# Late-query attention first in alternating pairs, and six blocks of layer one moved behind the attention at 512 tokens beside layer two's weight conversion

## The chip, the core and the metric

The kernel runs on one core of one Trainium2 chip. Its engines are TensorE (PE: matmuls, and the weight loads PEld that overlap them), VectorE (DVE), ScalarE (ACT), GpSimd (POOL) and SyncE (SP), which issues DMAs. Each runs its own queue of instructions in order; they meet through semaphores. The metric is the device time of the whole program in microseconds (us), the median of several executions. "L883" is line 883 of the kernel's file.

## What is computed

Attention with a memory term, causal, on four batches and eight heads, then two feed-forward layers on the 2304 tokens that come out. All data are float32, the weights of the two layers arrive as float64.

```python
# q, k, v: (4, 8, 576, 64)
scores = where(causal, -1e9, q @ k.T / 8);  a = softmax(scores)
local = a @ v
q_p = elu(q) + 1
mem_out = (q_p @ M_prev) / (q_p @ z_prev + 1e-6)
attn = g * mem_out + (1 - g) * local            # g = sigmoid(beta), by head
x = attn as (2304, 512)
h = x @ moe_w_in;   x = maximum(0.01 * h, h) @ moe_w_out       # layer one, 512 -> 2048 -> 512
h = x @ moe2_w_in;  out = (h - tanh(h)) @ moe2_w_out           # layer two, the same sizes
```

## The kernel before

**Attention** is cut into 32 units (class Unit, L453): two heads of one batch, with the first 256 queries (kind A, "early", 256 keys) or the last 320 (kind B, "late", all 576 keys). A unit's steps are: load of qk and v; the memory term (L546, finished by L565 and added by TensorE at L706); scores on TensorE (L608, and L613 for the last 64 queries) into PSUM tiles "s"; maxima with the mask on VectorE (L634), which also writes the scores to tiles "e"; exponentials on ScalarE (L654); scaling by the row sums (L688 to L692); transposes on TensorE (L740, L728) and copies to "pt"; the values on TensorE (L762) into PSUM "o". Four units of one kind and batch fill a block "x" of 256 tokens; the 64 queries left over of each batch make a ninth block, "R". Each "e" tile has one buffer, so a unit's scores find a place when the unit before has been transposed.

**A layer** multiplies a block by w_in (up), applies the activation and multiplies by w_out (down). Each float32 operand is held as two fp32r parts, high and low, and a product is three matmuls (high x high, high x low, low x high). The float64 weights come as pairs of 32-bit words; `convert` (L795) makes float32 of them with one magnitude on ScalarE (L820) and four VectorE instructions (L823, L826, L831, L836), then for layer one a high copy (L435, L437) and a low part (L448). Layer one's weights are 32 tiles of 512 KB. Layer two's are converted in 64 chunks of 256 columns into a DRAM scratch (vscr), and later reloaded and split.

**Layer one** is narrow: 256 tokens a time, a "pair" of two weight tiles being 24 up (L883) and 24 down matmuls (L985) with the leak (L962) between, eight pairs per block. The first four blocks go in two sweeps (SWEEPS; 2 pairs, then 6), with partial sums in DRAM, since their weights are not all there yet. Layer one's matmuls fill TensorE between the units' steps.

**What sets the order.** Nothing is ordered by the hardware but by the program's text, and that text comes from a planner (class Schedule): each step is an operation with its possible engines, its cost and its priority, and the planner plays the engines forward on these costs and emits what is ready. Units have the priority of their number; the weights' conversions are set between units by W1_FROM and W2_FROM; layer one takes what is left. RINGS gives the number of buffers.

**Layer two** is wide: a loop written by hand, 512 tokens a round (four rounds and one half round for R), one item per weight tile: 12 up matmuls of 512 columns (L1180), the activation on ScalarE and VectorE (L1148 to L1160), a high copy (L1167) and a low part on GpSimd (L448), and, three items later, 12 down matmuls (L1206). It begins when all of layer one is done.

Of the kernel before, what the change touches and what calls it, by code (L numbers as in the profile page):

```python
# [40 lines left out]
STEP = 8  # L41

FINE = (0, 0, 0, 0, 16, 48, 24, 40, 8, 32, 20, 28, 36)

APART = (160, 192, 160, 192, 192)
# [3 lines left out]
CALM = 6000.0  # L49

# [47 lines left out]
class Schedule:  # L98


    def __init__(self, rings):
        self.rings = {k: [None] * n for k, n in rings.items()}
        self.count = {k: 0 for k in rings}
        self.made = {k: 0 for k in rings}
        self.ops = []
        self.lanes, self.sent, self.landed = [0.0] * LANES, 0, 0.0

# [50 lines left out]

    def send(self, t, sizes):

        for size in sizes:
            k = self.sent % LANES
            t = max(t, self.lanes[k])
            took = size / 375.0
            self.landed = self.lanes[k] = max(self.landed + max(180.0, took), t + 2000.0 + took)
# [4 lines left out]
    def run(self):  # L170
# [13 lines left out]
        cold, mode = 0.0, 0  # L184
# [3 lines left out]
        while todo:  # L188
# [6 lines left out]
            while again:  # L195
                again = False
                for e in engines:
                    if free[e] > t:
                        continue
                    for i, (_, _, at, o) in enumerate(ready[e]):  # L200
# [12 lines left out]
                        if e == "pe":  # L213
# [3 lines left out]
                            if t > free[e] + 700.0:  # L217
                                cold = t
                            if t < cold + 3600.0:
                                mine += o.alts[e] + 90.0  # L220
# [40 lines left out]
CW = 256  # L261
# [9 lines left out]
W1_FROM, W1_STEP = (3.7, 15.7), 0.002  # L271

SPLIT = 4

CUT = 2
W2_FROM, W2_STEP = 14, 0.25
# [3 lines left out]
def kernel(  # L280
# [80 lines left out]

    chunks = [(m, f, c) for p in range(NP) for m in range(2) for f in (2 * p, 2 * p + 1) for c in range(512 // CW)]

# [15 lines left out]
    groups = [(k, b) for k in "AB" for b in range(B)]  # L379
# [13 lines left out]
    xsv = [dram.tile([128, KT, 256], F32, name=f"xsv{n}") for n in range(SPLIT)]  # L393
    xps = [dram.tile([128, KT, 256], F32, name=f"xps{n}") for n in range(SPLIT)]
    x8s = dram.tile([128, KT, 256], F32, name="x8s")

# [24 lines left out]
    x_h, mz_h = {}, {}  # L421
    w_h = [[sc.new(None) for f in range(NF)] for m in range(2)]
# [3 lines left out]
    xv_h = [sc.new(None) for n in range(NBLK)]  # L426
    xp_h = [[sc.new(None) for i in range(2)] for n in range(NBLK)]

    SWEEPS = [(n, 0, CUT) for n in range(SPLIT)] + [(n, CUT, NP) for n in range(SPLIT)]
    SWEEPS += [(n, 0, NP) for n in range(SPLIT, NBLK)]  # L430
# [22 lines left out]
    class Unit:  # L453
# [14 lines left out]
        def declare(self, pr, prev):  # L468
# [25 lines left out]
            fresh_mz = (kind, b) not in mz_h  # L494
            if fresh_mz:
                mz_h[kind, b] = new("mz")
            mz = mz_h[kind, b]
# [790 lines left out]
```

## Time and profile before

| | us |
|---|---|
| median of 3 runs | 1050.04 |
| lowest and highest | 1049.82, 1052.98 |
| the profiled execution | 1052.7 |
| its span, first to last instruction | 1051.0 |
| PE busy in the span | 1017.6 |
| DVE, ACT, POOL busy | 733.1, 615.4, 104.8 |
| first wide matmul of layer two | at 654.05 |

Busy times are sums over the span; a stretch with its own limit is read from the view by stretches. The durations of neighbouring instructions on an engine can overlap, so their starts tell what one costs. A view's "releaser" is what ended an engine's idle time.

### The profile page before, as it was taken

The numbers are of one execution on the slowest core, as the hardware profiler recorded it, in microseconds if no ns is written. First come the engines' busy times: TensorE is split into PE (matmuls) and PEld (weight loads), VectorE is DVE, ScalarE is ACT, GpSimd is POOL, SyncE is SP. The second block draws the span as 40 slices with busy tenths as digits, with TensorE's granted clock in tenths as the row PEclk, the third lists the DMA queues.
The fourth block names the chain that finished last, engine by engine and source line by source line (L and its number), as shares of the span: only waits on it lengthen the run. The fifth ranks groups of instructions, "written<-read, shape, count | busy, mean of one in ns | idle before, by whom it ended". The sixth has DMA issues, their size and how long they took to land.

```text
span 1051.0 us, 18406 instructions
## 1 busy us (share of the span) xinstructions
PE 1017.6 (97%) x6816; PEld 881.0 (84%) x6816; DVE 733.1 (70%) x1718; ACT 615.4 (59%) x1298; POOL 104.8 (10%) x111
## 2 busy tenths in 40 slices
PE   5789998999999999999999999999999999999998
PEld 3678897877779977989999999888888888888897
DVE  7999997786776667763212257788687687777765
ACT  6888875667562256553101123776676676676664
POOL 1000100000000000000000000222222222222221
PEclk9899999999999999999999999999999999999999
DMA  9765625544644354332100046000100010010010
GB/s 256 233 191 164 219 100 156 167 124 129 187 120 153 110 149 131 114 89 67 41 1 21 1 161 198 23 21 1 61 21 1 36 46 1 0 61 1 1 41 20
DMA packets 93866, 95.06 MB, mean 90 GB/s; under 512 B 45392, under 2 KB 69968, under 8 KB 93776
## 3 DMA queue, kind: packets, MB, share of 16 engines
q1 hardware_dynamic: 92560, 92.58, 28.9%
q10 hardware_dynamic: 1216, 1.31, 0.4%
q8 instruction: 53, 0.87, 0.3%
q14 instruction: 37, 0.30, 0.1%
HBM read 71.32 MB, written 22.54 MB: 89 GB/s over the span
## 4 chain that ended last, share of the span: by engine, by line
PE 76%; DMA 5%; ACT 2%; DVE 1%; issue 0%; SPq 0%; ACTq 0%
PE up L1180 19%; PE dn L1206 19%; PE dn L985 14%; PE up L883 14%; PE s L740 3%; PE o L762 3%; PE s L608 2%; DMA cv<-in_moe_w_in_dram 2%; PE s L613 1%; DMA qk<-in_qkt_dram 1%; PE s L546 1%; DMA vs<-cv 1%; PE o L706 1%; DMA cv<-in_moe_w_out_dram 1%; ACT cv L820 0%; PE s L728 0%
## 5 line engine op out<-in xcount | busy, mean ns | idle before, releaser
L883 PE MATMUL up<-xs,w 128*128 128x256 f32 x1728 | 233.4, 286 | 1.2 <-ACT g L962 1.2
L883 PEld LDWEIGHTS up<-xs,w 128*128 128x128 f32 x1728 | 216.2, 191 | 6.4 <-issue 5.0
L1180 PE MATMUL up<-xs,w 128*128 128x512 f32 (+1 forms) x960 | 207.7, 367 | 0.0
L1180 PEld LDWEIGHTS up<-xs,w 128*128 128x128 f32 x960 | 167.7, 188 | 30.4
L1206 PE MATMUL dn<-w,gh 128*128 128x512 f32 x576 | 174.9, 389 | 0.0
L985 PE MATMUL dn<-gh,w 128*128 128x256 f32 x1152 | 159.5, 284 | 0.3 <-DVE gh L437 0.3
L985 PEld LDWEIGHTS dn<-gh,w 128*128 128x128 f32 x1152 | 144.3, 189 | 4.8 <-issue 4.8
L448 POOL TENSOR_TENSOR gl<-gf,gh 128x512 fp32r<-128x512 f32 x71 | 92.0, 1296 | 485.9 <-ACT gh L1167 485.9
L1157 DVE SCALAR_TENSOR_TENSOR gf<-u,w 128x512 f32<-128x512 f32 x72 | 83.7, 1163 | 68.1 <-ACT w L1154 68.0
L962 ACT ACTIVATE g<-up 128x512 f32<-128x512 f32 x72 | 42.6, 594 | 144.6 <-PE up L883 138.6
L1206 PEld LDWEIGHTS dn<-w,gh 128*128 128x128 f32 x576 | 107.6, 188 | 21.8
L1206 PE MATMUL dn<-w,gl 128*128 128x512 f32 x288 | 109.5, 389 | 0.0
L654 ACT ACTIVATE e<-e,mx 128x128 f32<-128x128 f32 (+4 forms) x144 | 82.9, 578 | 18.7 <-DVE mx L634 10.7
L1148 ACT ACTIVATE u<-up 128x512 f32<-128x512 f32 x72 | 42.9, 596 | 79.5 <-PE up L1180 79.5
L985 PE MATMUL dn<-gl,w 128*128 128x256 f32 x576 | 82.7, 282 | 0.0
L437 DVE CAST gh<-g 128x512 fp32r<-128x512 f32 x32 | 13.7, 427 | 90.7 <-ACT g L962 90.7
L985 PEld LDWEIGHTS dn<-gl,w 128*128 128x128 f32 x576 | 73.4, 188 | 2.8 <-issue 2.8
L634 DVE CUSTOM_DVE_ANT_0 e<-s,mask 128x128 f32<-128x128 f32 (+4 forms) x144 | 64.0, 483 | 16.5 <-PE s L608 12.7
L740 PE MATMUL s<-identr,e 128*128 128x128 f32 x448 | 65.4, 284 | 7.8 <-DVE e L690 3.3
L435 ACT ACTIVATE pt<-s 128x320 f32<-128x320 f32 (+4 forms) x147 | 57.2, 435 | 18.7 <-PE s L740 10.2
L1206 PEld LDWEIGHTS dn<-w,gl 128*128 128x128 f32 x288 | 54.1, 188 | 11.4
L740 PEld LDWEIGHTS s<-identr,e 128*128 128x128 f32 x448 | 52.5, 145 | 12.3 <-ACT pt L435 4.4
(98 smaller groups left out, 1382.0 us busy)
## 6 DMA issues: line engine op xcount, KB each, us to landing
w<-in_moe_w_out_dram SPq DMA_DIRECT2D x16, 512.0 KB, 5.0
cv<-in_moe_w_in_dram SPq DMA_DIRECT2D x32, 256.0 KB, 2.8
vs<-cv SPq DMA_DIRECT2D x64, 128.0 KB, 1.8
cv<-in_moe_w_out_dram SPq DMA_DIRECT2D x32, 256.0 KB, 3.0
w<-vs SPq DMA_DIRECT2D x32, 256.0 KB, 2.8
w<-in_moe_w_in_dram SPq DMA_DIRECT2D x14, 512.0 KB, 5.1
qk<-in_qkt_dram SPq DMA_DIRECT2D x16, 448.0 KB, 3.8
v<-in_v_dram SPq DMA_DIRECT2D x16, 320.0 KB, 3.5
```

Source lines behind the costliest of these rows:

```text
L435: nc.scalar.activation(out=out, in_=in_, func=AF.Copy)
L448: (nc.vector if e == "dve" else nc.gpsimd).tensor_tensor(out=out, in0=in_, in1=high, op=ALU.subtract)
L634: nc.vector.tensor_tensor_reduce(out=out, in0=in0, in1=in1, scale=-scale, scalar=mx.tile[:, 0:1] if t == 4 and j else BIG, op0=ALU.add, op ...
L654: nc.scalar.activation(out=x, in_=x, func=AF.Exp, scale=-1.0, bias=mx.tile[:, k:k + 1], accum_out=sm.tile[:, 2 * i + j:2 * i + j + 1])
L740: nc.tensor.transpose(ss[j].tile[:, a:a + 128], x, ident)
L883: nc.tensor.matmul(ps()[:, s, :], lhsT=w[:, wh * 512 + kt * 128:wh * 512 + (kt + 1) * 128], rhs=xs()[:, xh, kt, :], start=(kt == 0 and j = ...
L962: nc.scalar.activation(out=g.tile, in_=ps.tile.rearrange("p a b -> p (a b)"), func=AF.Prelu, alpha=0.01)
L985: nc.tensor.matmul(dn[m // 2].tile[:, m % 2, :], lhsT=w[:, wh * 512 + m * 128:wh * 512 + (m + 1) * 128], rhs=gg.tile[:, s * 256:(s + 1) * ...
L1148: nc.scalar.activation(out=u, in_=h, func=AF.Square)
L1157: nc.vector.scalar_tensor_tensor(out=g, in0=u, scalar=lin, in1=w, op0=ALU.mult, op1=ALU.add)
L1180: nc.tensor.matmul(ps[:, s * n:(s + 1) * n], lhsT=w[:, wh * 512 + kt * 128:wh * 512 + (kt + 1) * 128], rhs=xs[:, xh, kt, 0:n], start=(kt = ...
L1206: nc.tensor.matmul(dn, lhsT=g[:, c0:c0 + 128], rhs=wt[1][f][:, wh * 512:(wh + 1) * 512], start=(fs[0] == 0 and s == 0 and j == 0), stop=(f ...
```

## The change

The units' list (UNITS) has the late kind first, then the early one, and the blocks are numbered in that order: B0 to B3, A0 to A3, R. The late units of batch 0 and all early units alternate between two sets of "e" tiles; the late ones' second set lies in three weight tiles (LENT) that are loaded later. The first six units (LEND) put their scores into layer one's PSUM tiles "up" and "dn" instead of "s".

Only three blocks (NARROW: B0, B1, B2) go through layer one narrow, in one sweep each. The other six are stored (x1s), and the hand-written loop gets three wide rounds of layer one before layer two's five. In the first 32 of their 48 items, two chunks of layer two's weights per item are loaded (`fetch`) and converted (`refine`) into the scratch; in the last 16 each weight tile is reloaded and split (`reload`) as soon as its last use is past. The planner's own clock model and DMA costs are changed too (pace, send), with W1_FROM, which sets the conversions of weight tiles 1 to 8 against the units.

```diff
-W1_FROM, W1_STEP = (3.7, 15.7), 0.002
-SPLIT = 4
+W1_FROM, W1_STEP = (7.7, 15.7), 0.002
+NARROW = 3
+LEND = 6
+LENT = ((0, 15), (1, 15), (1, 14))
+UNITS = [(k, b, hp, hp % 2 if k == "A" or b < 1 else 0) for k in "BA" for b in range(4) for hp in range(4)]
...
             for tiles in ([[0, 1]] if kind == "A" else [[2], [3], [4]]):
-                ss = [new("s"), new("s")]
+                if not self.lend:
+                    ss = [new("s"), new("s")]
+                elif tiles == [3]:
+                    ss = [new("dn0"), new("dn1")]
+                else:
+                    ss = [new("up"), new("up")]
...
-                    et[t - q0] = new(f"e{t if t > 1 or self.hp % 2 else t + 2}")
+                    if kind == "A":
+                        et[t - q0] = new(f"e{t if self.alt else t + 2}")
+                    else:
+                        et[t - q0] = new(f"{'h' if self.alt else 'e'}{t}")
...
+        if n >= NARROW:
+
+            def save_x(e):
+                nc.sync.dma_start(out=x1s[n], in_=x.tile)
+
+            sop([("sp", 600)], save_x, reads=[x], writes=[x1_h[n]], dma=[-524288])
+            return
...
-    for i, (m, f, c) in enumerate(chunks):
-        convert(m, f, c, 1, (0, 100 + i), [ends[min(int(W2_FROM + i * W2_STEP), len(ends) - 1)]])
-    for i, sweep in enumerate(SWEEPS):
-        layer1(i, *sweep)
+    for n in range(NBLK - 1):
+        layer1(n)
...
-    WIDE = SPLIT
-    rounds = [(2 * r, 2 * r + 1) for r in range(WIDE)] + [(NBLK - 1,)]
+    rounds = [(1, (NARROW + 2 * r, NARROW + 2 * r + 1)) for r in range((NBLK - NARROW) // 2)]
+    FIRST2 = len(rounds)
+    rounds += [(2, (2 * r, 2 * r + 1)) for r in range(NBLK // 2)] + [(2, (NBLK - 1,))]
...
+    def act1(i):
+        h = state.pop((2, i, "up"))
+        g = t_p.tile([128, 512], F32, name="gf")
+        nc.scalar.activation(out=g, in_=h, func=AF.Prelu, alpha=0.01)
+        if "late" in state:
+            act2_end(*state.pop("late"))
+        yield
+        state["late"] = (i, g)
...
+                    if layer == 1:
+                        lhs, rhs = w[:, wh * 512 + k * 128:wh * 512 + (k + 1) * 128], g
+                    else:
+                        lhs, rhs = g[:, c0:c0 + 128], w[:, wh * 512:(wh + 1) * 512]
...
+    def reload(m, f, step):
+
+        w = wt[m][f]
+        if step == 0:
+            nc.sync.dma_start(out=w.bitcast(F32)[:, 512:1024], in_=vscr[m][f])
+        else:
+            copy("act", w[:, 0:512], w.bitcast(F32)[:, 512:1024])
+            low("dve" if m else "pool", w[:, 512:1024], w.bitcast(F32)[:, 512:1024], w.bitcast(F32)[:, 0:512])
+
+    def fetch(j):
+        m, f, c = chunks[j]
+        raw = t_p.tile([128, 512], I32, name=("u", "hu")[j % 2])
+        w_load(raw, (w2_in, w2_out)[m], m, f, c, 256, nc.sync)
+        state["raw", j] = raw
+
+    def refine(j):
+        m, f, c = chunks[j]
+        raw = state.pop(("raw", j))
+        g = t_p.tile([128, 512], F32, name=("w", "mk")[j % 2])
+        for step in (c_abs, c_max, c_shift, c_high, c_low):
+            step(raw[:, :], g[:, 0:256])
+        nc.sync.dma_start(out=vscr[m][f][:, c * 256:(c + 1) * 256], in_=g[:, 0:256])
...
     for i in range(len(items) + LAG2):
...
+        for j in range((i + 1) * EACH, min((i + 2) * EACH, len(chunks))):
+            fetch(j)
+        for j in range(i * EACH, min((i + 1) * EACH, len(chunks))):
+            refine(j)
+        for turn in turns.get(i, ()):
+            reload(*turn)
```

How the instructions stand after the change, at three places. In a row, "x9" counts neighbours of the same form, the names are the output's and the inputs' tiles with a number of their making, and "128x256" is partitions by elements. In the kernel after, L910 and L988 are the narrow up and down (L883, L985 before), L647 and L652 the scores, L567 the memory term, L745 its addition, L779 and L767 the transposes, L801 the values, L1163 and L1200 the wide up and down.

TensorE around its first matmul of layer one, before (the values and transposes of early units, then the first up matmuls of weight tile 0):

```order
L762 MATMUL o<-pt,va 64x256 x2
L762 MATMUL o<-pt,va 64x128 x2
L740 MATMUL s<-identr,e_497 128x128
L740 MATMUL s<-identr,e_501 128x128 x2
L740 MATMUL s<-identr,e_497 128x128
L740 MATMUL s<-identr,e_501 128x128 x2
L883 MATMUL up<-xs,w_0_258 128x256 x9
L546 MATMUL s<-mz_168,ph 128x130 x2
L883 MATMUL up<-xs,w_0_258 128x256 x3
L883 MATMUL up<-xs,w_1_311 128x256 x12
```

Ahead of this piece stand only the first early units. TensorE at the same point after the change:

```order
L647 MATMUL up<-qk 128x384 x2
L647 MATMUL dn_928<-qk 128x512
L647 MATMUL dn_929<-qk 128x512
L767 MATMUL s<-identr,e_715 128x128
L567 MATMUL s<-mz_165,ph 128x130 x3
L652 MATMUL up<-qk 64x288 x4
L801 MATMUL o<-pt,v 64x320 x6
L801 MATMUL o<-pt,v 64x192 x2
L801 MATMUL o<-pt,v 64x64 x2
L910 MATMUL up<-xs,w_0_273 128x256 x9
L745 MATMUL o<-identr,mo 128x128 x3
L910 MATMUL up<-xs,w_0_273 128x256 x3
```

Before, 48 rows of attention stand ahead of the first up row, all of early units; now 138 rows do, those of five late units up to their values and the scores of the sixth, which go into "up" and "dn".

VectorE beside a late unit's maxima (L634 before, L673 after; "ISA e,mx" is a maximum), before, in the late half of the attention:

```order
L690 TENSOR_SCALAR e_3357<-e_3357,sm 128x576
L538 SCALAR_TENSOR_TENSOR ph<-qk,ph 128x320
L823 TENSOR_SCALAR cv<-cv 128x256
L826 TENSOR_SCALAR cv<-cv 128x256
L831 SCALAR_TENSOR_TENSOR cv<-cv 128x256
L634 ISA e_3490,mx<-s,mask 128x384
L634 ISA mx 128x1
L634 ISA e_3490,mx<-s,mask 128x384
L634 ISA mx 128x1
L836 SCALAR_TENSOR_TENSOR cv<-cv 128x256
```

The conversions between are chunks of layer two (256 columns). VectorE at a late unit's maxima after the change, in the first half of the attention (L841, L844, L849 and L854 are the conversion's four instructions, L468 the low part):

```order
L673 ISA e_1366,mx<-s,mask 128x384
L673 ISA mx 128x1
L673 ISA e_1366,mx<-s,mask 128x384
L673 ISA mx 128x1
L468 TENSOR_TENSOR w_6_1377<-cv,w_6_1377 128x512
L844 TENSOR_SCALAR cv<-cv 128x512
L841 TENSOR_SCALAR cv<-cv 128x512
L849 SCALAR_TENSOR_TENSOR cv<-w_7_878,cv 128x512
L709 SCALAR_TENSOR_TENSOR sm<-sm,omg_72 128x2
L844 TENSOR_SCALAR cv<-cv 128x512
L714 RECIPROCAL sm<-sm 128x2
L854 SCALAR_TENSOR_TENSOR cv<-w_7_878,cv 128x512
```

A late unit's own instructions are the same ones; beside them stand layer one's weight tiles (512 columns), all 32 by the twelfth unit's maxima, and no chunk of layer two anywhere in the attention.

TensorE at the end of the narrow layer one, after:

```order
L988 MATMUL dn_3965<-gl,w_15_2332 128x256 x2
L988 MATMUL dn_3978<-gl,w_15_2332 128x256 x2
L1163 MATMUL up<-xs,w_0_273 128x512 x12
L1163 MATMUL up<-xs,w_1_401 128x512 x12
L1163 MATMUL up<-xs,w_2_581 128x512 x12
L1163 MATMUL up<-xs,w_3_614 128x512 x12
L1200 MATMUL dn_5020<-gh,w_0_404 128x512 x2
L1200 MATMUL dn_5020<-gl,w_0_404 128x512
L1200 MATMUL dn_5021<-gh,w_0_404 128x512 x2
L1200 MATMUL dn_5021<-gl,w_0_404 128x512
L1200 MATMUL dn_5022<-gh,w_0_404 128x512 x2
L1200 MATMUL dn_5022<-gl,w_0_404 128x512
```

The last narrow down rows are followed by four groups of 12 wide up matmuls, and then by the wide down matmuls, in which a piece of the weight is the stationary operand; before, at this place, layer two's wide rounds began.

## Rows read from the trace of the kernel before

**Rows 1.** The page: busy time of two engines; granted clock in 40 slices, in tenths.
```profile
PE 1017.6 (97%) x6816; PEld 881.0 (84%) x6816; DVE 733.1 (70%) x1718; ACT 615.4 (59%) x1298; POOL 104.8 (10%) x111
...
PEclk9899999999999999999999999999999999999999
```

**Rows 2.** Stretches: length, busy PE, PEld, DVE, ACT, POOL (instructions), granted clock, DMA share, GB/s.
```profile
0.00:654.05 654.05, 625.04 (x4993) 552.56 (x4994) 440.52 (x1338) 343.57 (x846) 12.75 (x40) 0.99 0.43 130
0.00:78.00 78.00, 57.57 (x397) 45.76 (x397) 71.36 (x270) 62.08 (x183) 5.93 (x17) 0.93 0.79 229
26.00:52.00 26.00, 19.99 (x144) 16.09 (x141) 25.92 (x97) 21.84 (x65) 1.24 (x2) 0.87 0.79 234
...
78.14:109.86 31.72, 31.72 (x277) 27.76 (x276) 30.69 (x119) 26.80 (x83) 2.44 (x5) 1.00 0.51 148
195.51:260.00 64.49, 63.77 (x495) 50.14 (x494) 46.91 (x163) 45.43 (x114) 0.46 (x3) 1.00 0.49 141
654.05:1051.00 396.95, 392.56 (x1824) 328.48 (x1823) 292.58 (x380) 271.78 (x453) 92.03 (x71) 1.00 0.07 24
```

**Rows 3.** The same for narrow up matmuls alone (L883): PE, PEld, clock, DMA.
```profile
78.14:109.86 31.72, 11.17 (x75) 9.46 (x75) 1.00 0.51 148
195.51:260.00 64.49, 19.43 (x120) 15.84 (x120) 1.00 0.49 141
```

**Rows 4.** The same for narrow down matmuls alone (L985).
```profile
78.14:109.86 31.72, 8.29 (x60) 7.46 (x60) 1.00 0.51 148
195.51:260.00 64.49, 13.97 (x103) 12.65 (x102) 1.00 0.49 141
```

**Rows 5.** The chain that ended last: start, us, what; narrow, then wide.
```profile
483.92 2.80 PE dn L985 x24
486.72 2.80 PE up L883 x24
...
645.48 2.91 PE up L883 x24
...
664.96 2.72 PE dn L1206 x12
667.68 2.72 PE up L1180 x12
```

**Rows 6.** Timeline of VectorE: start, us, instruction.
```profile
139.51 0.69 DVE L836 SCALAR_TENSOR_TENSOR cv<-w,cv 128x512 int32<-128x512 int32 x1
140.11 0.69 DVE L448 TENSOR_TENSOR gl<-g,gh 128x512 fp32r<-128x512 f32 x1
140.72 0.42 DVE L826 TENSOR_SCALAR cv<-cv 128x512 int32<-128x512 int32 x1
141.05 0.69 DVE L448 TENSOR_TENSOR w<-cv,w 128x512 fp32r<-128x512 f32 x1
```

**Rows 7.** Groups of VectorE by form: count, busy us, mean ns, idle before.
```profile
L634 DVE CUSTOM_DVE_ANT_0 e<-s,mask 128x512 f32<-128x512 f32 x32 | 20.9, 686 | 1.7 <-PE s L608 1.5
...
L675 DVE RECIPROCAL sm<-sm 128x1 f32<-128x1 f32 x16 | 2.5, 159 | 0.2
```

**Rows 8.** Groups by form: leak, magnitude, one conversion, low part on GpSimd.
```profile
L962 ACT ACTIVATE g<-up 128x512 f32<-128x512 f32 x72 | 42.6, 594 | 144.6 <-PE up L883 138.6 <-DMA x2s<-g 5.5 <-DVE pt L437 0.2
...
L820 ACT ACTIVATE cv<-cv 128x256 f32<-128x256 f32 x64 | 27.7, 433 | 56.4 <-DMA cv<-in_moe_w_in_dram 25.8 <-DMA cv<-in_moe_w_out_dram 21.3 <-DVE gl L448 2.3
...
L831 DVE SCALAR_TENSOR_TENSOR cv<-cv 128x256 int32<-128x256 int32 x64 | 27.2, 424 | 1.5
...
L448 POOL TENSOR_TENSOR gl<-gf,gh 128x512 fp32r<-128x512 f32 x71 | 92.0, 1296 | 485.9 <-ACT gh L1167 485.9
```

**Rows 9.** Timeline of TensorE: a late unit's transposes that waited.
```profile
288.68 0.98 PE L740 MATMUL s<-identr,e 128*128 128x128 f32 x7 [1.77 <-ACT e L688]
```

**Rows 10.** Timeline of TensorE: six transposes at two times near the start.
```profile
39.48 1.75 PE L740 MATMUL s<-identr,e 128*128 128x128 f32 x6 [3.09 <-DVE e L690]
...
50.19 0.82 PE L740 MATMUL s<-identr,e 128*128 128x128 f32 x6
```

More of the change, by code (lines that the diff above doesn't have):

```diff
@@ L106, in __init__ @@
         self.lanes, self.sent, self.landed = [0.0] * LANES, 0, 0.0
+        self.speed, self.until, self.work = 0.5, 700.0 + WINDOW, []
     def new(self, tag):
@@ L157, in room, with pace @@
         return True
+    def pace(self, t):
+        while self.until <= t:
+            lo = self.until - WINDOW
+            busy = sum(min(b, self.until) - max(a, lo) for a, b in self.work if b > lo and a < self.until)
+            self.work = [x for x in self.work if x[1] > self.until]
+            if busy > 0.9 * WINDOW:
+                self.speed = 1.0
+            elif busy < 0.5 * WINDOW:
+                self.speed = 0.5
+            self.until += WINDOW
+        return self.speed
     def send(self, t, sizes):
@@ L376, in pool_copy @@
         nc.gpsimd.tensor_scalar(out=out, in0=in_, scalar1=1.0, scalar2=0.0, op0=ALU.mult, op1=ALU.add)
-    groups = [(k, b) for k in "AB" for b in range(B)]
+    groups = []
+    for u in UNITS:
+        if u[:2] not in groups:
+            groups.append(u[:2])
+    groups.sort(key=lambda g: max(i for i, u in enumerate(UNITS) if u[:2] == g))
     blocks = groups + [("R", 0)]
@@ L425 @@
     x2_h = [sc.new(None) for n in range(NBLK)]
[L426 to L430, printed above, removed]
+    x1_h = {n: sc.new(None) for n in range(NARROW, NBLK - 1)}
+    x1_h[NBLK - 1] = x8_h
     seqs = [0]
@@ L869, in convert, with w_lo @@
+        def w_lo(e):
+            w = wt[m][f]
+            low(e, w[:, 512:1024], g.tile, w.bitcast(F32)[:, 0:512])
+        op(copies(512), w_hi, reads=[g], writes=[wh])
+        op(lows(512), w_lo, reads=[g, wh], writes=[wh])
         return first
@@ L1049 @@
     ends = []
-    for kind, b in groups:
-        for hp in range(H // 2):
-            u = Unit(kind, b, hp)
-            u.declare((0, u_at), prev)
-            prev = u
-            u_at += 1
-            ends.append(sc.ops[-1])
+    for kind, b, hp, alt in UNITS:
+        u = Unit(kind, b, hp)
+        u.alt, u.lend = alt, u_at < LEND
+        u.declare((0, u_at), prev)
+        prev = u
+        u_at += 1
+        ends.append(sc.ops[-1])
     att_ops = list(sc.ops)
@@ L1087, in load2 @@
         x = late["x2"].tile([128, KT, 256], F32, name="x2i")
[L1088 removed]
+        layer, parts = rounds[r]
+        nc.sync.dma_start(out=x, in_=(x1s if layer == 1 else x2s)[parts[i]])
         state[2, r, i, "x"] = x
@@ L1184, in token_tiles @@
     def token_tiles(r):
-        return [(n, t) for n in rounds[r] for t in range(2)]
+        return [(n, t) for n in rounds[r][1] for t in range(2)]
     def out_copy(r, k):
-        n, t = token_tiles(r)[k]
+        layer, parts = rounds[r]
         last = r == len(rounds) - 1
@@ L1196, in down2 @@
         r, fs = items[i]
+        layer = rounds[r][0]
         if fs[0] == 0:
@@ L1213, in down2 @@
                 out_copy(r, k)
-    items = [(r, (f,)) for r in range(WIDE) for f in range(NF)]
-    items += [(WIDE, (2 * p, 2 * p + 1)) for p in range(NP)]
+    items = [(r, (f,)) for r in range(len(rounds) - 1) for f in range(NF)]
+    items += [(len(rounds) - 1, (2 * p, 2 * p + 1)) for p in range(NP)]
     def prep2(r, step):
-        if r + 1 < len(rounds) and step // 2 < len(rounds[r + 1]):
+        if r + 1 < len(rounds) and step // 2 < len(rounds[r + 1][1]):
             i = step // 2
@@ L1231 @@
             up2(i)
-            steps = act2(i)
+            r, fs = items[i]
+            steps = act1(i) if rounds[r][0] == 1 else act2(i)
             next(steps)
```

259 lines of the change are left out of this document (112 added, 147 removed), and 2 rows, old and new, of the table RINGS.

## The prediction

> **What bounds the kernel now.** I read the page's busy times first, then the view by stretches, then single rows. The page [rows 1] has TensorE at 97% of the span, with no other engine over 70%, and its line of granted clock is at full speed but for one or two slices at the start. The stretches [rows 2] say where the other 3% lie. Up to 654.05 us (attention and layer one) TensorE is busy 625.04, so 29.0 us are idle; 20.4 of these lie in the first 78 us, where VectorE is busy 71.4 of 78.0. From 654 on (layer two, 512 tokens wide) 392.6 of 397.0 are busy. So a gain must come from fewer TensorE microseconds, or from the start.
>
> What the units cost TensorE follows from one stretch of each kind, cut at the start of a unit's values. From 195.51 to 260.00 there are four late units, and in the same stretch 120 narrow up and 103 narrow down matmuls [rows 2 to 4]. A narrow matmul goes by at 2.80/24 = 0.1167 us [rows 5] (the printed duration is longer, since they overlap), so (64.5 - 0.7 idle - 223 x 0.1167)/4 = 9.4 us for a late unit. From 78.14 to 109.86 there are five early units and 135 narrow matmuls: (31.7 - 15.8)/5 = 3.2. The attention is then 16 x 9.4 + 16 x 3.2 = 202 us; a block's layer one is 8 x 48 x 0.1167 = 44.8, nine are 403. Together 605: of the 654 us 49 are lost, 29 to idling and some 20 to a low clock, to broken rows of matmuls and to my rounding.
>
> VectorE needs the same care. Its printed durations overlap: 139.51, 140.11, 140.72 and 141.05 are successive starts, so a row of 0.69 costs 0.60 and one of 0.42 costs 0.335 [rows 6], 0.085 less than printed. A weight tile of layer one is 2 x 0.335 + 3 x 0.60 = 2.47. A late unit has 15 groups of instructions of its own, 114.5 us in 310 over 16 units, of which the first and the last stand in [rows 7]: (114.5 - 310 x 0.085)/16 = 5.5, with a copy now and then 5.6.
>
> **The change part by part.**
> (1) Six blocks pass layer one wide. A wide group of 12 takes 2.72, so 0.2267 a matmul [rows 5]. One 512-token round is 16 x 5.44 = 87.0, three are **261.1**; narrow, the same six blocks are 6 x 44.8 = 268.8. The gain is 7.7, up to 3.5 more where groups take 2.91 instead of 2.80, as the row at 645.48.
> The Trainium skill's "TensorE: Matmul & The Clock Gate", section "Wait — 56ns, not 53.3ns?", gives N/2.4 GHz plus about 2.5 ns from start to start. By it a pair of 256 columns costs 2.6 ns more than one of 512, an estimate of 3.0 us over 1152; the rows give 6.7 ns a pair, and they decide.
>
> (2) The conversion of layer two's weights leaves the attention and lies in the first two wide rounds, two chunks per item of 5.44 us. Per item VectorE gets 8 instructions of at most 0.424 (3.4), ScalarE the leak, a copy of the same size (0.594 each) and two magnitudes of 0.433 (2.1), GpSimd one low part of 1.296 [rows 8]. All lie under 5.44 us. In the last 16 items the reload puts another 0.7 to 1.3 on these engines, still under. I cost this at nothing; TensorE's rows are the cover, and if an engine went over the item, say VectorE by 0.5 us, 32 items would cost 16. In the attention VectorE loses 64 conversions, though TensorE idled there hardly.
>
> (3) The partial sums of four blocks, their DRAM trips and the second splits go: no TensorE work, beside which they lay.
>
> (4) Late units come first. This is the dear part: before any layer-one matmul, TensorE's order now has five late units and the start of the sixth, 48 us of work, where it had nine early ones. What ends the wait is VectorE: in its order five late units (28.0), 9 1/4 weight tiles (22.9) and the sixth unit's maxima with the first splits (5) stand ahead of the second split, **56 us**. In the first 26 us VectorE of before lost 5.7 (71.36 + 6.64, nearly all of it before 26 [rows 2]), so the floor is 56 + 8 = 64, with the set-up. DMA does not set it: 9 1/4 tiles of 512 KB and six units of 768 KB are 9.6 MB, 41 us at the 234 GB/s of [rows 2]. A late unit is a chain through three engines (scores, maxima, exponentials, scaling, transposes, values), at the start of which VectorE has only tiles that DMA has brought: I take 6 us more, about what it lost in before, **70 us**. The upper end is TensorE at half clock, below. Alternating score tiles and the scores in the free up and down banks are there from the first unit; without them the chains would not overlap.
>
> (5) What is left for TensorE then: 16 x 9.4 + 16 x 3.2 + 3 x 44.8 - 48 = **288 us**. Next come units six to eleven: up to the last weight tile VectorE has six units (33.6), 22 3/4 tiles (56.2) and layer one's splits (6), 96 us; TensorE has in the same place six units (56.4) and some 357 narrow matmuls (41.7), 98, nearly a tie. One wait by a late unit for ScalarE's scaling was 1.77 us, with two more of 0.3 behind it [rows 9]; I put 1 us on each of ten late units and 5 on the rest, **15**. The ends are 5 (0.7 were idle in four late units [rows 2]) and 29.
>
> **The sum.** 70 + 288 + 15 = 373 for the attention stage, 261.1, and 397.0 as it was: a span of 1031. The profiled execution took 1052.7 with a span of 1051.0, so 1.7 lie around it; the median of the runs is 1050.04, 2.7 under that execution. 1031 + 1.7 - 2.7 = **1030 us**. So 49 us of loss become 22 + 15 + some rounding, and 8 come from the width. The attention stage breaks even at 654 - 261 = 393 us.
>
> **The rivals.**
> B, the start is tight: VectorE stays full from 8 us on (25.92 of 26 from 26 to 52 [rows 2] says that it can) and the late units wait little. 64 + 288 + 5 = 357, span 1015, **1014 us**. Against it: VectorE's order must match the arrival of work from TensorE and ScalarE, and with nothing but late units in flight TensorE cannot fill holes.
>
> C, slower: **the half clock holds through the five late units.** Six transposes took 1.75 us at 39.48, behind 3.09 us in which TensorE idled, and 0.82 at 50.19 [rows 10]; the granted clock of 26 to 52 was 0.87. Without layer-one matmuls TensorE's work comes in pieces with gaps between, and at 1.2 GHz 48 us become 96, so TensorE itself sets the start: 97 instead of 70 us, span 1058, **1057 us**. It decides from a start of 90 us on. For it: those two rows. Against: at 50.19 the clock was back while layer-one matmuls were still few. Nor need it matter: VectorE's 64 us are longer than the 48 at full clock, and a start in which half of the work runs at either clock costs 24 + 48 = 72, little over my 70.
> The Trainium skill's same page, section "Part 1: The HAM clock gate", says that the throttled clock is the default and activity releases it; the two rows agree with that (slow behind an idle stretch, fast behind matmuls), and by it alone the gaps between late units would bring C.
>
> D, the same time: **VectorE costs what is printed.** The overlap of 0.085 us is from a stretch where it ran without waits. If it is lost to waits for semaphores, 56 becomes 73 and 96 becomes 119: 81 instead of 70, and 119 instead of 98 + 10, together 22 more, span 1053, **1052 us**. Against it: 163 instructions in 46.9 us beside 64.5 with hardly an idle TensorE [rows 2].
>
> That the conversion does not hide (part 2) is no case of its own; it lengthens the tail of each by up to 16.
>
> **How the numbers follow.** A measurement of this kernel can tell about 0.3%, or 3.2 us, from no change: faster is under 1046.9, slower over 1053.2. The forecast (A), 1020 to 1042: 0.55. B: 0.17. D: 0.14, of which 0.11 falls within 0.3% and 0.03 below. C: 0.14. Faster 0.55 + 0.17 + 0.03 = 0.75, same 0.11, slower 0.14. The range runs from just under B to C, 1013 to 1057: what lies below B's time and above C's is about half of their chances, 0.15.
>
> **What would show it.** The first narrow up matmul at about 70 us: 64 speaks for B, 90 and more for C with transposes of six at 1.7 us, 80 with a VectorE that has no gaps for D. The first wide matmul at 373; the first layer-two matmul 261 us later, with VectorE, ScalarE and GpSimd under 70% there and no idle TensorE; 397 us from there to the end. If wide groups of 12 take over 2.72, or TensorE waits for "gh", "gl" or a weight tile between 373 and 634, part 2 was wrong. If the start is long but the clock full and VectorE has gaps, it is the latency of a late unit's chain that I set too low at 6 us.

## The result

The changed kernel took 1019.26 us, the median of four runs (1018.21 to 1019.87), beside 1049.93 for the kernel before on the same chip: a ratio of 0.970 (95% interval 0.968 to 0.973), 30.7 us faster where 20 were forecast. Its profiled execution has a span of 1017.4 us.

The page, as in [rows 1]: busy time by engine and the granted clock in 40 slices.

```profile
PE 995.1 (98%) x5664; PEld 817.5 (80%) x5664; DVE 702.8 (69%) x1592; ACT 629.6 (62%) x1325; POOL 196.9 (19%) x174
...
PEclk9999999999999999999999999999999999999999
```

The stretches of the changed kernel answer to [rows 2]: length, busy PE, PEld, DVE, ACT, POOL, clock, DMA share, GB/s. They are the start, the rest of the attention, layer one wide, layer two, and the attention as a whole.

```profile
0.00:70.34 70.34, 55.05 (x362) 34.16 (x363) 64.96 (x220) 56.89 (x141) 8.25 (x23) 0.98 0.72 213
70.34:359.36 289.02, 286.35 (x2331) 238.73 (x2328) 207.93 (x713) 199.65 (x531) 7.46 (x16) 1.00 0.33 95
359.36:620.40 261.04, 261.04 (x1153) 216.09 (x1153) 137.85 (x281) 102.81 (x204) 86.99 (x63) 1.00 0.47 150
620.40:1017.40 397.00, 392.66 (x1825) 328.50 (x1823) 292.04 (x379) 270.29 (x451) 94.18 (x73) 1.00 0.08 26
...
0.00:359.36 359.36, 341.40 (x2689) 272.88 (x2690) 272.89 (x932) 256.54 (x671) 15.71 (x39) 1.00 0.40 118
```

The cuts come from TensorE's timeline and from the chain that ended last (start, us, what): the first narrow up matmul, then the first wide ones and the pace of 2.72 us that [rows 5] show for layer two.

```profile
70.34 1.32 PE L910 MATMUL up<-xs,w 128*128 128x256 f32 x9
```
```profile
359.36 10.93 PE up L1163 x48
370.29 2.72 PE dn L1200 x12
373.01 2.72 PE up L1163 x12
```

From 70 us on TensorE idles 2.7 us in all until layer two; the view of waits (what waited for what, us in total, times, longest) has this much of it:

```profile
PE s L779 <- ACT e L727: 1.8, 2, 1.1
PE s L779 <- ACT pt L455: 0.5, 2, 0.3
PE dn L988 <- ACT gh L455: 0.4, 1, 0.4
```

| term | forecast | measured |
|---|---|---|
| first narrow up matmul | 70 | 70.3 |
| TensorE's work from there to the wide rounds | 288 | 286.4 |
| idle beside it | 15 | 2.7 |
| layer one wide | 261.1 | 261.0 |
| layer two | 397.0 | 397.0 |
| span | 1031 | 1017.4 |
| from span to the median of the runs | -1.0 | +1.9 |

### The profile page after: what moved, and what is told of

The parts are those of the page before. It is cut to its first block, busy times and chain, and to the rows that moved or that the text cites. A ratio compares the mean times of both kernels' runs of the same rounds, so it can differ in the third digit from the quotient of the medians.

```text
span 1017.4 us, 16055 instructions
## 1 busy us (share of the span) xinstructions
PE 995.1 (98%) x5664; PEld 817.5 (80%) x5664; DVE 702.8 (69%) x1592; ACT 629.6 (62%) x1325; POOL 196.9 (19%) x174
## 4 chain that ended last, share of the span: by engine, by line
PE 91%; DVE 5%; DMA 2%; ACT 1%; issue 1%; SPq 0%; ACTq 0%
PE up L1163 32%; PE dn L1200 32%; PE up L910 6%; PE dn L988 6%; PE o L801 4%; PE s L779 4%; PE s L647 3%; DMA qk<-in_qkt_dram 2%; PE s L567 1%; PE o L745 1%; PE s L652 1%; DVE e L673 1%; DVE cv L849 1%; DVE w L673 1%; DVE e L729 0%
## 5 line engine op out<-in xcount | busy, mean ns | idle before, releaser
L1163 PE MATMUL up<-xs,w 128*128 128x512 f32 (+1 forms) x1536 | 346.1, 375 | 0.0
L1163 PEld LDWEIGHTS up<-xs,w 128*128 128x128 f32 x1536 | 275.8, 188 | 52.9
L468 POOL TENSOR_TENSOR gl<-gf,gh 128x512 fp32r<-128x512 f32 x119 | 154.9, 1301 | 591.7 <-ACT gh L1150 579.5
L1200 PE MATMUL dn<-w,gh 128*128 128x512 f32 x576 | 174.8, 389 | 0.0
L1200 PEld LDWEIGHTS dn<-w,gh 128*128 128x128 f32 x576 | 107.6, 188 | 22.0
L1200 PE MATMUL dn<-gh,w 128*128 128x512 f32 x384 | 118.3, 389 | 0.0
L1200 PE MATMUL dn<-w,gl 128*128 128x512 f32 x288 | 109.5, 389 | 0.0
L693 ACT ACTIVATE e<-e,mx 128x256 f32<-128x256 f32 (+4 forms) x134 | 76.0, 569 | 21.8 <-DVE mx L673 13.6
L910 PE MATMUL up<-xs,w 128*128 128x256 f32 x576 | 86.8, 290 | 0.0
L1150 ACT ACTIVATE gh<-gf 128x512 fp32r<-128x512 f32 x120 | 74.6, 621 | 16.9 <-DVE gf L1143 16.8
L1200 PEld LDWEIGHTS dn<-gh,w 128*128 128x128 f32 x384 | 72.1, 188 | 15.0
L910 PEld LDWEIGHTS up<-xs,w 128*128 128x128 f32 x576 | 73.6, 189 | 4.7 <-issue 4.7
L1200 PE MATMUL dn<-gl,w 128*128 128x512 f32 x192 | 74.7, 389 | 0.0
L1200 PEld LDWEIGHTS dn<-w,gl 128*128 128x128 f32 x288 | 54.0, 188 | 11.3
L673 DVE CUSTOM_DVE_ANT_0 e<-s,mask 128x128 f32<-128x128 f32 (+4 forms) x114 | 46.8, 455 | 22.3 <-PE s L647 19.3
L779 PE MATMUL s<-identr,e 128*128 128x128 f32 x404 | 56.9, 279 | 4.4 <-ACT e L727 1.8
L1143 DVE COPY_PREDICATED gf<-mk,up 128x512 f32<-128x512 int32 x72 | 53.7, 746 | 7.4
L988 PE MATMUL dn<-gh,w 128*128 128x256 f32 x384 | 54.7, 286 | 0.4 <-ACT gh L455 0.4
```

Of the source, the lines that this page charges most:

```text
L468: (nc.vector if e == "dve" else nc.gpsimd).tensor_tensor(out=out, in0=in_, in1=high, op=ALU.subtract)
L673: nc.vector.tensor_tensor_reduce(out=out, in0=in0, in1=in1, scale=-scale, scalar=mx.tile[:, 0:1] if t == 4 and j else BIG, op0=ALU.add, op ...
L693: nc.scalar.activation(out=x, in_=x, func=AF.Exp, scale=-1.0, bias=mx.tile[:, k:k + 1], accum_out=sm.tile[:, 2 * i + j:2 * i + j + 1])
L779: nc.tensor.transpose(ss[j].tile[:, a:a + 128], x, ident)
L910: nc.tensor.matmul(ps()[:, s, :], lhsT=w[:, wh * 512 + kt * 128:wh * 512 + (kt + 1) * 128], rhs=xs()[:, xh, kt, :], start=(kt == 0 and j = ...
L988: nc.tensor.matmul(dn[m // 2].tile[:, m % 2, :], lhsT=w[:, wh * 512 + m * 128:wh * 512 + (m + 1) * 128], rhs=gg.tile[:, s * 256:(s + 1) * ...
```

## The experiments

Spans are those of each run's profiled execution, to be held against 1051.0 before and 1017.4 after; ratios are to the kernel before, run on the same chip. Beside these runs the spans of the kernel before went from 1047.6 to 1054.1, so a difference of one to three microseconds between two single spans tells nothing.

### What the order gives, and what the width

**e9_order_alone** and **e12_order_one_sweep** put the late units first into the kernel before. "Order" here takes in what came with it: the lent and alternating tiles and the planner's costs, which no run separates.

```diff
 # e9, on the kernel before: UNITS, lent tiles, Schedule and W1_FROM of the changed kernel; then
-            halves = [sc.new("e0"), sc.new("e1")]
+            halves = [sc.new("z0"), sc.new("z0")]
 # e12, on e9
-    SWEEPS = [(n, 0, CUT) for n in range(SPLIT)] + [(n, CUT, NP) for n in range(SPLIT)]
-    SWEEPS += [(n, 0, NP) for n in range(SPLIT, NBLK)]
+    SWEEPS = [(n, 0, NP) for n in range(NBLK)]
```

> The kernel before with the order alone: late units first with the alternating score tiles, the lent PSUM tiles and the changed planner costs; all nine blocks still go through layer one narrow, four of them in two sweeps, and layer two's weights are still converted beside the attention. (The second sweeps load their tokens into one tile of their own, and early units have one value tile, so that the memory suffices.) Theory O (the order lessens the loss by itself): the stage up to layer two falls from 654 to 628 to 636 us, the time to 1024 to 1032. Rival W (the order pays only where six blocks leave the attention): the stage falls by less than 8 us, the time is 1042 or more.

Ratio 1.019 (1.017 to 1.021), span 1069.5. Theory O is out; the number lies in W's "1042 or more", though W had not said that the order could cost time. The start was as in the changed kernel, but in the stretch behind it TensorE idled 21.4 us and ran at a clock of 0.92:

```profile
70.00:240.00 170.00, 148.59 (x1007) 108.31 (x1005) 138.56 (x418) 119.88 (x290) 5.04 (x15) 0.92 0.41 120
```

A block of late tokens is ready only every four late units, and in two sweeps it gives two of its eight pairs to fill the gaps. That this was the cause is a reading; the next run tests it. (It also gives the early units their second value tile back, which e9 lacked; behind 240 us, where the early units lie, TensorE idled only 2.8 us of 420 in e9.)

> The kernel before with the order alone, as the run e9_order_alone, but each of the nine narrow blocks in one sweep over all eight pairs, as the changed kernel has them (and both value tiles back). In e9 the loss lay between 70 and 240 us, where TensorE idled 21.4 us: with two sweeps a block offers only two of its eight pairs until four blocks are there. Theory F (late units first pay only if each block gives all its layer one as filler at once): the stage up to layer two is 605 us of work and a loss of 23 to 30, 628 to 635, the time 1026 to 1033, under the kernel before by 19 to 26. Rival W (the order pays only with six blocks out of the attention): the loss stays over 45, the time is 1048 or more.

Ratio 0.985 (0.982 to 0.989), span 1034.4, 16.6 under the kernel before; layer two began at 637.29. Theory F's range was missed by 4 us and W is out: the order gives its part without the wide rounds, once a block is all filler. One sweep with the early units first was not run over nine narrow blocks, so the order's part and the single sweep's are not told apart. Two stretches of e12:

```profile
0.00:637.29 637.29, 617.89 (x4993) 545.17 (x4994) 443.88 (x1346) 331.42 (x817) 12.78 (x37) 0.99 0.41 121
...
71.30:637.29 565.99, 560.12 (x4635) 509.87 (x4632) 378.78 (x1127) 274.49 (x677) 4.42 (x14) 1.00 0.37 110
```

This splits the gain. Before and e12 have the same 4993 matmuls [rows 2], of 625.04 and 617.89 busy us: 7.2 us less for the same matmuls, 9.6 less idle (29.0 to 19.4), 16.8 together (by the ratios, which rest on several executions, some 15 of 31 in all). From e12 to the changed kernel another 17.0: six blocks took 560.1 - 286.4 = 273.8 us of TensorE narrow and take 261.0 wide, **12.7**; the idle behind the start fell from 5.9 to 2.7; the start from 71.3 to 70.3.

**e4_halves** has the width by itself.

```diff
-                        rhs=xs[:, xh, kt, 0:n], start=(kt == 0 and j == 0), stop=(kt == KT - 1 and j == 2))
+                    parts = 2 if rounds[r][0] == 1 else 1
+                    for c in range(parts):
+                        nn = n // parts
...
+                            rhs=xs[:, xh, kt, c * nn:(c + 1) * nn], start=(kt == 0 and j == 0 and c == 0),
...
```

The down matmuls are halved in the same way.

> The changed kernel with each 512-column matmul of layer one's three wide rounds written as two of 256 columns (2304 in place of 1152), the order of the rest unchanged. By the rows of the kernel before (0.1167 us for a narrow one, 0.2267 for a wide one) the three rounds take 3 x 16 x 48 x 0.1167 = 268.8 instead of 261.0 us, the time rises by 7.7 us. By the estimate of 2.6 ns a pair from the Trainium skill's page on TensorE (TensorE: Matmul & The Clock Gate) it rises by 3.0 us. If the second half, which needs no new weights, goes by at the wide one's rate, by 0.

Ratio 0.984 (0.983 to 0.986), span 1033.1, 15.7 more than the changed kernel. The chain shows why it is neither 7.7 nor 3.0:

```profile
371.02 2.88 PE dn L1208 x24
373.90 2.88 PE up L1166 x24
```

24 halves take 2.88 us, 0.120 each, where [rows 5] had 0.1167 for the quicker narrow ones: 16 x 3 x 5.76 = 276.5 against 261. So 512 columns are worth 7.7 to 15.5 us for six blocks. What makes 256 columns cost 0.117 in one place and 0.120 in another was not tried. One candidate stands in the stretches: each half had a weight load of its own (2312 beside 2313 matmuls, so the third guess, of a second half without new weights, does not apply), and the loads filled the time, while at 512 columns they took 216.09 of 261.04 us.

```profile
359.36:640.00 280.64, 280.64 (x2313) 279.39 (x2312) 143.57 (x286) 106.43 (x212) 88.66 (x65) 1.00 0.44 140
```

**e1_early_first** undoes the order in the changed kernel, and with it W1_FROM and the late units' second set of tiles.

```diff
-UNITS = [(k, b, hp, hp % 2 if k == "A" or b < 1 else 0) for k in "BA" for b in range(4) for hp in range(4)]
+UNITS = [(k, b, hp, hp % 2 if k == "A" else 0) for k in "AB" for b in range(4) for hp in range(4)]
-W1_FROM, W1_STEP = (7.7, 15.7), 0.002
+W1_FROM, W1_STEP = (3.7, 15.7), 0.002
```

> The changed kernel with the units' order undone: early units first, then late ones (W1_FROM back to 3.7, a single set of score tiles for late units); three narrow blocks (now A0 to A2), six wide ones and the conversion in the wide rounds stay. Theory O (the order gives most): the attention stage of the changed kernel was 359 us where its TensorE work at full clock is 336, a loss of 23; the kernel before lost 49, of which some 36 in the first 78 us with early units first. So with early units first the stage loses 36 to 49 again: 372 to 385 us, the time 1032 to 1045. Theory R (the relief of VectorE and ScalarE from layer two's weights, and the wide rounds, give it, whatever the order): the stage stays within 4 us of 359, the time 1015 to 1023.

Ratio 1.040 (1.037 to 1.043), span 1093.4: theory O's direction, several times its size; the wide rounds began at 433 us instead of 359. The price was not only at the start. TensorE idled 21.1 us in the first 78, 14.0 from there to 250 and 26.5 from 250 to 433, where the changed kernel idled 18.0 in its whole attention. Layer one's narrow matmuls were over at 350 us, and the last late units ran bare, their values in the chain 13 to 15 us apart, about what a late unit of the changed kernel takes with filler beside it (198.0, 212.9 and 228.0 us), and at a clock of 0.87; then layer one's first wide round had nothing in front to hide its load and split:

```profile
360.67 2.21 PE o L801 x20
...
374.75 2.21 PE o L801 x20
...
390.09 2.21 PE o L801 x20
...
404.28 2.21 PE o L801 x20
...
421.49 3.65 DMA x2i<-x1s
425.24 1.06 ACT xs L455
426.33 1.24 DVE xs L1094
427.58 3.35 DMA x2i<-x1s
```
```profile
345.00:421.50 76.50, 61.34 (x363) 40.98 (x359) 36.33 (x133) 42.08 (x108) 0.76 (x5) 0.87 0.21 58
```

**e8_narrow1** takes the filler away in the changed order.

```diff
-APART = (160, 192, 160, 192, 160, 192, 160, 224)
+APART = (160, 192, 160, 192, 160, 192, 160, 192, 224)
...
-NARROW = 3
+NARROW = 1
```

APART holds a place in memory for each wide round's tokens; there is one round more.

> The changed kernel with one narrow block and eight wide ones in four rounds. The attention loses 90 us of TensorE's work and the wide rounds gain 87.0, so it breaks even at an attention stage of 272 us. If the loss stays at 23 us the stage takes 269 and the time falls by 3. If the late units now run bare (13 to 14 us each, as the last ones did in e1_early_first, against 15 to 18 with filler beside them) the stage takes 290 to 310 and the time rises by 18 to 38 us; I expect this.

Ratio 1.017 (1.013 to 1.020), span 1065.6. The wide rounds began at 318.3 instead of the 272 of break-even; TensorE idled 28.3 us of the last 118 at a mean clock of 0.90, and again waited for the first split. The mean hides three pieces: the last late units bare (0.86, up to about 245 us), early units bare (1.00), and the wait.

```profile
200.00:318.30 118.30, 90.00 (x624) 59.98 (x622) 76.20 (x352) 81.94 (x263) 0.30 (x2) 0.90 0.38 106
...
200.00:250.00 50.00, 40.69 (x247) 27.07 (x247) 27.99 (x118) 30.74 (x90) 0.30 (x2) 0.86 0.25 67
250.00:300.00 50.00, 44.39 (x348) 29.87 (x345) 43.24 (x223) 44.97 (x159) 0.00 (x0) 1.00 0.47 128
```
```profile
PE up L1163 <- ACT xs L455: 12.0, 1, 12.0
```

I expected 18 to 38 us more and it was 48. The units themselves came out as expected, the last values ending at 305 us, within 290 to 310; the rest is the wait for the first split, which I had not counted.

### What sets the start

**e5_less_dve**: VectorE loses 32 instructions, the rest keeps its place.

```diff
-        op([("dve", DVE(512))], step(c_low), reads=[raw, g], writes=[g])
+        op([("dve", DVE(512))], lambda e: None, reads=[raw, g], writes=[g])
```

> The changed kernel with one of VectorE's four conversion instructions left out in each of layer one's 32 weight tiles (the one that puts in the lowest three bits of the fraction), the order of all other instructions on every engine as it was. Theory V (VectorE sets the start): about 9 of them lie ahead of the first narrow up matmul, 9 x 0.60 = 5.4 us, so that moves from 70.3 to about 65 and the time falls by 4 to 6 us; the others lie beside a TensorE that is never idle and give nothing. Theory L (the late units' chain, or DMA, sets it): the start moves by under 2 us and the time by under 2. If VectorE bound the middle too, the fall would be nearer to 19 us.

Ratio 0.967 (0.965 to 0.969), span 1016.5, 0.9 less. The first up matmul came at 68.68: of 5.4 us taken from VectorE, an estimate, 1.7 came back.

```profile
68.68 1.32 PE L910 MATMUL up<-xs,w 128*128 128x256 f32 x9
```

Theory V's 4 to 6 us did not come. In other runs with the same start that matmul came at 69.9 to 71.4 us (e6, e8, e9, e11 and e12), so the 1.7 is uncertain by about 1. **e2_one_set**, **e3_no_lend** and **e10_alt_two** change the tiles that a late unit holds and no work, though the planner lays out the order anew in each:

```diff
 # e2: one set of score tiles for all late units;  e10: two sets for batches 0 and 1
-... hp % 2 if k == "A" or b < 1 else 0 ...
+... hp % 2 if k == "A" else 0 ...
+... hp % 2 if k == "A" or b < 2 else 0 ...
 # e3: scores of the first six units in "s"
-LEND = 6
+LEND = 0
```

> The changed kernel with one set of score tiles for all late units (no alternation in batch 0). In the changed kernel the first late units' values follow one another at 11.6, 11.6, 8.2 and 8.5 us; with a single set the shortest distance seen in the kernel before was 13.0. Theory L (a late unit's chain sets the start): five units at 13 or more, so the first narrow up matmul moves from 70.3 to 77 to 84 us and the time rises by 5 to 14 us. Theory V (VectorE sets the start, with 65.0 us busy of 70.3): it gets other work (weight tiles) in the gaps, the first up matmul moves by under 4 us, and the time by under 4.

Ratio 0.979 (0.977 to 0.981), span 1028.6.

> The changed kernel without the lent PSUM tiles: the first six units' scores go to the three tiles s, as all others do. Theory L (the chain of a late unit sets the start): two units share three tiles, the first narrow up matmul moves from 70 to 73 to 78 us, the time rises by 2 to 8 us. If the score tiles in SBUF alone decide (e2_one_set), it stays within 2 us.

Ratio 0.983 (0.979 to 0.986), span 1033.4.

> The changed kernel with the late units of batch 1 alternating too, as those of batch 0 do. Theory L (a late unit's chain through its score tiles sets the start, as one set for all cost 11 us): units five and six no longer wait for each other, so the first narrow up matmul comes 2 to 4 us earlier than 70.3 and the time falls by 1 to 4 us. Theory V (VectorE sets it): no change, within 1 us.

Ratio 0.968 (0.967 to 0.970), span 1015.3. The first up matmuls of e2, e3 and e10, in this order:

```profile
84.61 1.32 PE L910 MATMUL up<-xs,w 128*128 128x256 f32 x9
```
```profile
83.72 3.07 PE L910 MATMUL up<-xs,w 128*128 128x256 f32 x24
```
```profile
67.83 0.95 PE L910 MATMUL up<-xs,w 128*128 128x256 f32 x6
```

With fewer tiles the first up matmul came 14.3 and 13.4 us later, and the spans followed by 11.2 and 16.0. This is theory L's direction, but e3 goes far beyond the range given for it (73 to 78, and 2 to 8 us). In e2 the late units' values start 13.4, 14.4, 11.3 and 14.0 us apart; in the changed kernel the distances are 11.6, 11.6, 6.8 and 9.9 (the expectation's 8.2 and 8.5 are misread). VectorE is busy 78.0 of 84.6 us in e2, since the planner put more weight tiles into the gaps, but only 69.2 of 83.7 in e3, so there it is not full; part of e3's delay is TensorE's clock, 0.83 from 40 to 60 us, where the changed kernel had 1.00.

e10 supports nothing. Its first up matmul stands ahead of the fifth late unit's values instead of behind them, so its 2.5 us are another order and not an earlier unit: these values came later than in the changed kernel. First e10, then the changed kernel:

```profile
69.52 2.28 PE L801 MATMUL o<-pt,v 128*64 128x320 f32 x20
```
```profile
68.14 2.27 PE L801 MATMUL o<-pt,v 128*64 128x320 f32 x20
```

e10 has the lowest span of all, 2.1 us less, and an interval that overlaps the changed kernel's. So fewer tiles lengthen the start, and more were not shown to shorten it.

### What hides the conversion

**e6_conv_inside** puts it back beside the attention, in the way of the kernel before.

```diff
+    for i, (m, f, c) in enumerate(chunks):
+        convert2(m, f, c, (0, 100 + i), [ends[min(int(14 + i * 0.25), len(ends) - 1)]])
...
-        for j in range((i + 1) * EACH, min((i + 2) * EACH, len(chunks))):
-            fetch(j)
-        for j in range(i * EACH, min((i + 1) * EACH, len(chunks))):
-            refine(j)
```

> The changed kernel with the conversion of layer two's weights put back beside the attention (64 chunks from the end of unit 14 on, four per unit, as in the kernel before), and none in the wide rounds; everything else as changed. Theory O: TensorE idled only 8.6 us behind 78 us in the kernel before with these conversions beside it, and 2.7 behind 70 us now, so the attention stage grows by 0 to 6 us and the wide rounds stay at 261 us: the time rises by 0 to 6. Theory R (the relief is what counts): the stage grows by over 10 us.

Ratio 1.097 (1.095 to 1.099), span 1152.1, and both theories missed: the attention stage ended at 362.0, 2.6 us later, as theory O had it, but then TensorE waited once for 126.4 us.

```profile
PE dn L1229 <- ACT gh L1179: 126.4, 1, 126.4
```

ScalarE's first high copy of the wide rounds stood behind the magnitudes of the last chunks. In the chain a place in the ring of buffers comes round in 6.6 us, 4.4 of them DMA (a load and a store):

```profile
378.11 2.73 DMA cv<-in_moe_w_out_dram
...
382.52 0.44 DVE cv L854
382.98 1.69 DMA vs<-cv
...
384.72 2.52 DMA cv<-in_moe_w_out_dram
```

Two chunks share such a round, so a chunk costs 3.3 us even with ScalarE and VectorE idle most of the time: 41 magnitudes (L838) in the 137 us in which TensorE mostly waited (length, ScalarE's busy time and count, clock, DMA share, GB/s).

```profile
362.00:499.00 137.00, 17.53 (x41) 0.56 0.38 120
```

The 64 magnitudes took from 238.6 to 497.9 us. The kernel before did its 64 between 163.7 and 475.9, well inside its stage of 654 us; here only some 123 us were left between their start and the end of the stage. What VectorE's relief gave is read from e12 instead: with all 64 chunks beside the attention TensorE idled 5.9 us behind the start, so theory R is out.

**e11_no_prefetch** turns two lines round in the wide rounds, **e7_narrow5** does the same and has four chunks an item.

```diff
+        for j in range(i * EACH, min((i + 1) * EACH, len(chunks))):
+            refine(j)
         for j in range((i + 1) * EACH, min((i + 2) * EACH, len(chunks))):
             fetch(j)
-        for j in range(i * EACH, min((i + 1) * EACH, len(chunks))):
-            refine(j)
```

> The changed kernel with one thing turned round in the wide rounds: each item converts its two chunks before it issues the loads of the next two (they were issued before). Work per item is the same. Theory P (an item of lead for the loads is what hides the conversion; without it the loads queue on SyncE behind stores that wait for VectorE, ScalarE waits at a magnitude for about 3 us of DMA, and the high copy that TensorE needs stands behind it in ScalarE's queue): TensorE waits 1 to 4 us in most of the 32 items, the time rises by 30 to 100 us. Theory C (there is room for it: TensorE's items are 5.44 us and each engine's work under 3.4): under 5 us.

Ratio 1.048 (1.044 to 1.052), span 1102.5, 85.1 more: theory P. Waits of ScalarE and of SyncE's queue from 365 to 540 us:

```profile
ACT w L838 <- issue: 89.7, 15, 6.9
```
```profile
SPq L1243 <- DVE mk L841: 89.3, 22, 4.7
```

SyncE sits at a store (L1243) that waits for VectorE, the next loads stand behind it, ScalarE's magnitude (L838) waits for them (the view names no releaser for most of this; that it is the loads follows from the order), and behind that stands the high copy. TensorE's own waits make up 52 us, 13 of them for copies of layer one's results; the clock of 0.90 from 364 to 555 makes the rest plausible, but it was not separated.

> The changed kernel with five narrow blocks and two wide rounds of layer one; all of layer two's 64 chunks are converted in 16 items, four an item (each item converts its chunks before the next ones are loaded). Two blocks more are narrow: 89.6 us against 87.0 wide, the time rises by 2.6 us if the conversion still hides: on VectorE four chunks are 4 x 1.09 = 4.4 us by starts (16 instructions at 0.085 less than printed), under the item's 5.44. If its printed durations count (5.7 us) TensorE waits 4 to 6 us more. If DMA sets it (four loads of 256 KB and four stores of 128 KB in 5.44 us are 289 GB/s, more than any slice of the page shows), TensorE waits 10 us or more in these 16 items.

Ratio 1.052 (1.050 to 1.054), span 1106.9, with ScalarE waiting 32.1 us for "u" from w_out and 30.0 from w_in. Since it has e11's turned lines, it cannot tell whether VectorE or DMA would bound four chunks an item; that stays open.

## Why the prediction was right, and where not

The measured 1019.26 lies just under the 1020 to 1042 of the main forecast and nearer to rival B's 1014 than to 1030. The stages came in the order and nearly at the times that the prediction gives; one term, the idle time, was mis-sized.

**The start, 70 us: right by its size and nearly by its terms, wrong in what ended it.** I let VectorE set it, 56 us of its work ahead of the second split, 8 lost and 6 for the chain. In the changed kernel's chain VectorE does hold nearly every piece from 10 to 62 us, as here:

```profile
42.00 0.39 DVE ph L559
42.38 0.60 DVE w L673
...
42.99 0.60 DVE w L673
```

Up to 62.28 us it was busy 57.0 and idle 5.3. But TensorE did not wait for the second split. From there on it had 8.1 us of the fifth and sixth units' rows in its own order, without a gap, and the second split had ended at 65.4, 5 us ahead of the first up matmul. TensorE's stretch, and the split:

```profile
62.28:70.34 8.06, 8.05 (x59) 4.99 (x60) 7.99 (x27) 7.16 (x21) 0.15 (x1) 1.00 0.66 203
```
```profile
64.69 0.68 DVE L468 TENSOR_TENSOR xs<-x,xs 128x512 fp32r<-128x512 f32 x1
```

So the 6 us that I put on waits in "a chain through three engines" were 8.1 us of TensorE's work that I had not priced there, and that the sum met 70.3 is in part luck. It fits that 5.4 us less of VectorE's work brought 1.7 (e5), and that tiles without any work moved the start by 14.3 and 13.4 (e2, e3): I read this as several limits that lie close together, VectorE being one; which of them ends each step was not separated further. One reading in part 4 is wrong and enters no term: in the kernel before, the values of four early units, not nine, stand ahead of the first up matmul (at 40.88 us); nine are done by 78.

**The idle time behind it: the mis-sized term.** I took a wait of one row [rows 9], 1.77 us, and put 1 us on each of ten late units and 5 on the rest. The stretch in [rows 2] had said otherwise: 29.0 - 20.4 = 8.6 us idle in 576 after the start, 4.3 in 289. It was 2.7. These 12.3 us are nearly all of the span's miss of 13.7; the nearly tied VectorE (96 to 98, and the last weight tile came 99 us behind the start) cost nothing, since TensorE nearly always had a narrow matmul. Rival B had this term at 5; its start of 64 was wrong.

**The width, 7.7 to 11.2: low, by what it replaces.** The wide rounds took the 261.1 forecast. What they replaced was 273.8 us in place (e12) rather than 268.8: I priced the narrow blocks at their best rows. The estimate from the Trainium skill's "TensorE: Matmul & The Clock Gate", section "Wait — 56ns, not 53.3ns?", is 2.5 ns a pair by N/2.4 GHz plus about 2.5 ns, so 2.9 us, not 2.6 and 3.0. It is far under the 15.7 us of e4.

**The conversion, hidden at no cost: right,** with TensorE busy 261.04 of 261.04 us there. But the cover that I named (work per engine under 5.44 us) is not sufficient. e11 has the same work and loses 85 us. A further condition is the item's lead of the loads in SyncE's queue, past which I looked: I had summed the engines and not the queue.

**The rivals.** C did not come: the clock of the first 70 us was 0.98, with 0.94 up to 26 us and 1.00 from there. In e12, e9 and e8, with the same start, it was 0.93 to 0.95, and the first up matmul still came at 71.3, 69.9 and 70.5. A lower clock came elsewhere, where late units ran bare (0.87 in e1, 0.86 in e8) or nearly so (0.92 in e9). D is out: the last of 32 weight tiles was converted at 169.6 us, 99 behind the start, where VectorE's starts gave 96 and printed durations alone would have filled 119. VectorE's starts are what counts. By the Trainium skill's "Vector Engine (DVE) Microarchitecture Reference", section "5.2 Measured stream behaviour on trn2 (trn3 not measured)", an instruction costs 1.0417 ns a column and about 75 ns. An estimate from it is 608 ns for 512 columns, which agrees with the 0.60 of [rows 6] for instructions with two inputs; behind the one with a single input there (L826) the next starts after 0.33, which the estimate does not give.

**The offset.** The profiled execution of the kernel before lay 2.7 us over the median; that of the changed one did not, and so 2.9 us of the miss were given back.

## What to carry to other kernels

A filler decides an order: late units first pay when each block then gives its eight pairs at once (e12); the same order with two of eight pairs a block at first lost 18 us. It also leaves the cheap early units for the place where filler runs out: in e8 these ran bare at a full clock, the late ones did not. When idle time is to be forecast, scale the idle time of a whole stretch that has the same filler, not one row's wait; without the filler the scale does not hold (21.4 us in 170 in e9). And before work is called hidden, walk the in-order queues (the DMA issuer's too) for who stands behind whom: a sum of busy times does not see it.

## What the runs showed of the hardware

Matmuls of 256 columns take 0.1167 us in one place and 0.120 in another, at a full clock (e4), while 512 columns take 0.2267 in every full round. In both kinds of 256-column stretch the weight loads were busy nearly all the time (22.40 of 22.40 us at the end of the changed kernel's narrow blocks, 279.39 of 280.64 in e4). And the granted clock fell to 0.86 (e8, from 200 to 250 us) where late units ran without filler and TensorE waited again and again for a scaling, up to 1.6 us at a time; with filler beside the same units it stayed at 1.00, and so it did where early units ran without filler (e8, from 250 to 300 us).
